# DeltaNet and multiplicative FFN on one Trainium2 core: signs of converted weights taken from VectorE to ScalarE's parametric ReLU, and a new order of the steps

## The chip, the cores and the metric

The kernel runs on one core of a Trainium2 chip. Its time is the device time of one execution in microseconds (us). Five engines matter: TensorE (PE in the profile, its weight loads PEld), VectorE (DVE), ScalarE (ACT), GpSimd (POOL) and SyncE (SP), which issues nearly all DMAs from one queue.

## What is computed

The first half is a delta-rule attention over 768 tokens, for 4 batches and 8 heads of 48 features, with a 48 x 48 state per head. The second half is an FFN without activation functions, over 3072 tokens of 384 features:

```python
k_n = k / (norm(k) + 1e-6)
for t in range(768):
    y[t] = q[t] @ state
    v_old = state^T k_n[t]
    state = state + beta[t] * outer(k_n[t], v[t] - v_old)
x = y as (3072, 384)
out = ((x @ w1) * (x @ w2)) @ w3 @ w_out     # w1, w2: 384 x 1024; w3: 1024 x 1024; w_out: 1024 x 384
```

q, k, v and beta are fp32. The four weight matrices arrive as fp64, eight bytes an element, and the kernel converts them itself.

## The kernel before

**Attention.** The tokens go in 12 chunks of 64. Chunks are taken in pairs j. For each chunk m the program has steps, each a Python generator that issues a few instructions between two `yield`s:

- `k`, `q`, `v` load tiles by tokens, `p` loads permuted tiles of k and q (in eight small DMAs each). `K` and `Q` transpose chunks 0 and 1 on TensorE, `d` transposes the later ones on VectorE.
- `g` sums squares of k for a pair (POOL squares, DVE sums, a small matmul across halves), `N` makes the norms of a pair on DVE (some 14 small instructions) and sends a product across halves, `n` scales v by the norm.
- `s` makes the scores of a chunk (L367, L373) and the matrices U (DVE, L379) and PT. `u` stores U to DRAM in blocks.
- `V` inverts triangular 32 x 32 blocks of a pair: Ub is loaded back (L426), 31 steps of two DVE instructions each (L440, L445), for the first two pairs in PSUM with ScalarE copying in (L434) and out (L449), and Vd is stored. `e` loads the blocks (TT, T22), transposes on DVE (L481), and makes the off-diagonal corner with two sets of matmuls (L498) and ScalarE copies (L514, L525).
- `c` is the serial chain of a chunk: product of the state with k, R = v - that (DVE, L584), product with TT, X (DVE, L594), product with k, new state (DVE, L613 or L615). All these products are L551. `y` makes the outputs (L652) and ScalarE copies them to xT (L673), with a few DMAs.

**Weights.** Each matrix goes in pieces `P`: P0 to P7 are w_out (128 x 384), P8 to P23 w3 (128 x 512), P24 to P29 w1 and P30 to P35 w2. A piece has four steps, one on each of four engines: the load by SyncE into one of five `raw` tiles (a ring), two ScalarE passes (L707 on the high words, L708 on the low words), two VectorE passes (L710 shifts the exponent into place, L711 brings the sign in from the high word), and an integer add on GpSimd (L715). The fifth piece ahead has to be past its add before SyncE can issue the next load.

**FFN.** w3 @ w_out is folded once: `t` transposes a w3 piece on TensorE (L750), ScalarE copies it (L753), `f` multiplies (L759, 128 matmul records), ScalarE copies the result (L766). w_out stands in the tile of w2 (w2s) while it folds. Then, for each pair u of chunks and each of eight column blocks, `a` (and `b` for chunk 0 alone) makes x @ w1, copies it on ScalarE (L791), makes x @ w2 (both L779) and multiplies on VectorE (L795). The product with the folded matrix uses seven block products instead of eight: `T` (weight sums) and `S` (slab sums, L846) run on GpSimd, `o` on TensorE (L874), `x` puts the results together and stores them (L891, L905 to L911).

**Order.** The string `ORDER` lists the steps, one token for each `yield`. The program issues them in this order, and `in_text_order` then ties the instructions of each engine to that order. So ORDER sets the order on each engine, SyncE's queue among them; between the engines only semaphores wait. PSUM has two tiles of two banks (`ps_w`) and four of one bank (`ps_f`), taken in turn; slabs are ten, taken in turn.

Of the kernel before, what the change touches and what calls it, by code (L numbers as in the profile page):

```python
# [8 lines left out]
FP32 = mybir.dt.float32  # L9
# [30 lines left out]
beta k0 P0 g0 P13 P10 P0 k1 P18 beta K0 P0 P0 P12 P13 P13 q0 P10 P18 P10 P10 K0 K0 P13 K0 beta  # L40
K0 g0 g0 q1 P8 P1 P18 g0 P12 P18 P12 K1 g0 k2 K1 K1 K1 g0 g0 P12 Q0 K1 Q0 Q0 g0 Q0 g0 P5 g0 N0
Q0 Q1 P8 P8 s0 t5 Q1 Q1 g1 Q1 Q1 s1 g1 s0 P8 g1 P9 s0 s1 s1 s1 s0 t4 t2 s0 p2 P1 P5 s0 s0 s1 s1
V0 P11 P5 P5 N0 P3 t5 P1 P1 d2 u0 P9 d2 u1 P11 P3 P9 P4 P11 N0 P3 t4 P4 P4 P9 P11 t3 t2 P2 P7
P2 P14 t0 P7 P3 P2 V0 V0 t10 P6 s1 P2 P14 t3 V0 P7 V0 V0 V0 P6 f1 g1 p3 P4 P7 t0 P14 P6 P6 P16
V0 V0 P15 V0 V0 V0 f2 V0 t10 P16 P16 f2 P15 f1 V0 f1 P16 P19 V0 V0 p2 t1 V0 P19 P19 V0 V0 f2 f0
P14 t6 t1 f0 f0 V0 P15 V0 P19 V0 v0 P15 t6 s1 P20 d2 V0 P17 P20 P20 t11 V0 P17 t11 d2 V0 t8 t8
P20 V0 k3 g1 g1 V0 g1 f5 P17 t7 V0 P17 V0 P22 P22 f5 V0 t7 V0 f5 v1 n0 V0 f3 V0 V0 s0 f3 P23
P26 V0 g1 f4 d3 t9 V0 t9 V0 d3 f4 P22 P22 f3 t14 P23 P23 P24 P24 P26 p3 t14 d3 f4 P23 n0 P30
P24 P24 s2 V0 p4 e0 g1 g1 t15 t12 f7 t15 f7 t12 f6 P26 P26 N1 e0 e0 s2 s2 P21 d3 e0 P30 e0 e0
s2 f7 s2 P25 e1 s2 c0 P21 e1 e1 e1 c0 n1 s3 P21 P21 N1 s3 y0 y0 P31 N1 s3 s3 s3 P25 P25 s3 n1  # L50
P31 c0 c0 P25 V1 P30 u2 t13 u3 P32 P30 V1 t13 e1 e1 c1 P31 V1 f6 f6 c1 c1 c1 y1 y0 b1 P32 P32
P32 y1 V1 V1 V1 b0 V1 P31 V1 b0 b2 V1 V1 b1 V1 V1 P27 P27 b1 V1 P27 V1 b1 b2 P29 P29 V1 b3 b3
P29 y1 b3 a03 V1 P28 V1 b3 P27 a01 a02 c1 a03 V1 a00 V1 k4 V1 P29 P28 P28 a01 a00 V1 V1 a00 P28
a02 a05 a00 V1 b5 V1 a05 b6 V1 V1 V1 V1 P35 p4 P35 b6 P33 a07 V1 V1 V1 V1 V1 V1 g2 a07 a04 b5
a04 b7 P33 k5 a06 b4 b7 v2 n2 a01 V1 P35 P33 a06 P34 a03 c1 V1 a03 V1 b2 V1 P35 P33 g2 P34 P34
P34 e2 b2 a01 c2 d4 d4 g2 p5 b4 b0 a04 d4 g2 g2 b0 g2 g2 e2 a07 a06 g2 g2 a04 d4 e2 n2 c2 a07
V2 b4 a06 e2 e2 e2 b5 c2 g2 N2 s4 c2 b4 S0 s4 s4 a02 a02 c2 c2 p5 T b5 T y2 b6 y2 d5 T b7 d5 d5
e3 e3 d5 N2 s4 s4 s4 N2 b7 e3 e3 v3 a05 T u4 a05 s5 b6 S0 s5 s5 S0 s5 s5 n3 o0 x0 e3 e3 s5 c3
n3 c3 S0 u5 S0 S0 S0 S0 o0 S0 S0 S0 S0 c3 c3 o0 V2 y3 x0 o0 V2 S0 V2 S0 V2 V2 V2 o0 V2 y3 V2 k6
x0 S0 g3 c3 g3 g3 S0 g3 V2 v4 x0 o0 V2 V2 V2 y3 V2 a10 a10 x0 x0 k7 x0 o0 V2 x0 x0 a17 V2 V2 V2  # L60
V2 x0 V2 V2 V2 a17 V2 V2 a15 V2 V2 a13 a16 V2 V2 v5 V2 a13 p6 V2 a16 V2 a15 V2 g3 V2 a13 g3 a13
p6 x0 a14 c3 a14 V2 e4 d6 a10 a17 a12 e4 e4 e4 g3 g3 c4 a17 g3 d6 a10 a14 d6 a12 n4 n4 c4 e4 g3
e4 e5 n5 a12 c4 a11 d6 N3 a14 c4 c4 n5 a11 y4 p7 p7 c4 e5 s6 a11 s6 s6 y4 a15 a12 a11 c5 e5 V3
# [26 lines left out]
def kernel(  # L90
# [452 lines left out]
    def chain(c):  # L543
# [30 lines left out]
        R = nv  # L574
# [470 lines left out]
```

## Time and profile before

| what | value |
|---|---|
| median of 3 runs | 609.26 us (609.08 to 610.2) |
| span of the profiled execution, first to last instruction | 607.4 us |
| median of the runs less that span | 1.9 us |
| PE busy | 550.0 us (91%) |
| DVE busy | 364.9 us (60%) |
| ACT busy | 158.9 us (26%) |
| POOL busy | 177.2 us (29%) |
| mean granted TensorE clock | 0.966 |
| DMA | 57.31 MB, 90 GB/s of HBM traffic over the span |

The profiled execution has no time of its own beside its span; the 1.9 us is what lies around the span by the median. "Busy" is time with an instruction in the engine. A group is given as line, engine, operation, output and input tiles with shapes, count, then busy us and mean ns of one, then the idle time of the engine just ahead of them and what ended it. In the chain of waits each row is a start, a length and what was running. In the table by stage each engine's busy us is followed by the number of instructions.

### The profile page before, as it was taken

How to read it: one execution, taken by the hardware profiler on the slowest of the kernel's cores; microseconds unless marked ns; L12 is line 12 of the kernel's file. 1: busy time of each engine (PE TensorE's matmuls, PEld its weight loads, DVE VectorE, ACT ScalarE, POOL GpSimd, SP SyncE). 2: the span in 40 equal slices, each digit the busy share in tenths (PEclk: the TensorE clock that was granted, in tenths of full speed). 3: DMA queues.
4: the chain of work that ended last, by engine and by line, in shares of the span. 5: the costliest groups of instructions: out<-in, count | busy, mean ns of one | idle time of the engine just before them, and what ended most of it. 6: DMA issues, size and time to landing. Idle time of an engine off the chain costs nothing.

```text
span 607.4 us, 19078 instructions
## 1 busy us (share of the span) xinstructions
PE 550.0 (91%) x8188; PEld 383.1 (63%) x8188; DVE 364.9 (60%) x828; ACT 158.9 (26%) x333; POOL 177.2 (29%) x223
## 2 busy tenths in 40 slices
PE   2648789678898999999999989999999999999997
PEld 2545455657777885456964559745588545984477
DVE  3768977466998489765489463894764843311012
ACT  3645534445323111222111221121112012321100
POOL 6554443122255530304420016013053000600041
PEclk9988979669999999999999999999999999999999
DMA  9968998554956347462443534435323040010001
GB/s 192 244 155 226 186 189 173 97 133 94 165 104 88 82 92 120 92 98 39 101 101 73 81 52 87 97 70 103 58 51 84 31 85 5 5 52 13 1 0 52
DMA packets 219507, 57.31 MB, mean 94 GB/s; under 512 B 206656, under 2 KB 212800, under 8 KB 219424
## 3 DMA queue, kind: packets, MB, share of 16 engines
q1 hardware_dynamic: 215232, 55.31, 45.3%
q10 hardware_dynamic: 4192, 0.79, 0.9%
q8 instruction: 64, 1.05, 0.8%
q14 instruction: 19, 0.16, 0.1%
HBM read 43.88 MB, written 11.01 MB: 90 GB/s over the span
## 4 chain that ended last, share of the span: by engine, by line
PE 75%; DVE 8%; DMA 5%; issue 4%; ACT 3%; SPq 3%; ACTq 0%; DVEq 0%
PE ps_f L779 37%; PE ps_f L874 16%; PE ps_w L551 5%; PE ps_f L759 4%; PE ps_w L652 4%; DMA raw<-in_moe_w_dram 3%; PE ps_w L498 3%; PE ps_w L367 2%; DVE tb L440 2%; PE ps_w L373 2%; SPq L230 2%; DVE ps_w L445 2%; DMA ktok<-in_k_dram 1%; ACT xT L673 1%; PE ps_f L750 1%
## 5 line engine op out<-in xcount | busy, mean ns | idle before, releaser
L779 PE MATMUL ps_f<-xT,w2s 128*128 128x512 f32 (+1 forms) x336 | 133.7, 544 | 1.6 <-issue 1.5
L779 PE MATMUL ps_f<-xT,w1s 128*128 128x512 f32 (+1 forms) x336 | 128.7, 533 | 4.5 <-DVE ab L795 2.0
L846 POOL TENSOR_TENSOR ab<-ab 128x256 f32<-128x256 f32 x96 | 67.2, 729 | 195.0 <-DVE ab L795 171.0
L779 PEld LDWEIGHTS ps_f<-xT,w1s 128*128 128x128 f32 x336 | 63.0, 190 | 60.3 <-issue 52.0
L779 PEld LDWEIGHTS ps_f<-xT,w2s 128*128 128x128 f32 x336 | 63.2, 193 | 56.2 <-issue 52.3
L791 ACT COPY ab<-ps_f 128x512 f32<-128x512 f32 (+1 forms) x56 | 28.4, 525 | 172.7 <-PE ps_f L779 161.4
L874 PE MATMUL ps_f<-w,ab 128*128 128x192 f32 x376 | 66.5, 330 | 0.0
L874 PEld LDWEIGHTS ps_f<-w,ab 128*128 128x128 f32 x376 | 61.1, 190 | 4.4 <-issue 3.5
L795 DVE TENSOR_TENSOR ab<-ab,ps_f 128x512 f32<-128x512 f32 (+1 forms) x56 | 33.2, 605 | 49.1 <-PE ps_f L779 49.0
L440 DVE TENSOR_TENSOR tb<-Vb,Ub 128x31 f32<-128x31 f32 (+15 forms) x124 | 46.0, 371 | 15.5 <-DMA Ub<-Ud 12.1
L759 PE MATMUL ps_f<-w2s,w3T 128*128 128x384 f32 x128 | 48.4, 535 | 5.7 <-ACT w3T L753 5.0
L445 DVE TENSOR_TENSOR Vb<-Vb,tb 128x31 f32<-128x31 f32 (+15 forms) x124 | 47.2, 381 | 4.3
L874 PE MATMUL ps_f<-room,ab 128*128 128x192 f32 x272 | 47.9, 330 | 1.1 <-DVE room L905 1.1
L874 PEld LDWEIGHTS ps_f<-room,ab 128*128 128x128 f32 x272 | 44.1, 190 | 1.9 <-issue 1.5
L673 ACT COPY xT<-ps_w 48x256 f32<-48x256 f32 x96 | 30.4, 365 | 48.1 <-PE ps_w L652 47.5
L759 PEld LDWEIGHTS ps_f<-w2s,w3T 128*128 128x128 f32 x128 | 26.2, 211 | 24.2 <-ACT w3T L753 5.5
L270 POOL TENSOR_TENSOR sq<-ktok 128x384 f32<-128x384 f32 x24 | 20.9, 875 | 61.4 <-DMA ktok<-in_k_dram 30.1
L367 PE MATMUL ps_w<-KQ 48*64 48x128 f32 x384 | 31.3, 308 | 3.9 <-issue 2.0
L379 DVE TENSOR_TENSOR U<-ps_w,wt 128x512 f32<-128x512 f32 x24 | 16.6, 690 | 29.9 <-PE ps_w L373 28.6
L715 POOL TENSOR_TENSOR w<-w,raw 128x512 uint32<-128x512 uint32 x16 | 20.7, 1299 | 43.6 <-DVE w L711 18.6
L373 PE MATMUL ps_w<-KQ 48*64 48x64 f32 x768 | 32.1, 242 | 0.3 <-issue 0.3
L537 POOL TENSOR_TENSOR vtok<-vtok,n 128x384 f32<-128x384 f32 x24 | 20.1, 851 | 41.0 <-DMA vtok<-in_v_dram 26.8
(109 smaller groups left out, 676.4 us busy)
## 6 DMA issues: line engine op xcount, KB each, us to landing
raw<-in_moe_w_dram SPq DMA_DIRECT2D x16, 512.0 KB, 6.2
vtok<-in_v_dram SPq DMA_DIRECT2D x24, 192.0 KB, 4.3
raw<-in_moe_w_dram SPq DMA_DIRECT2D x24, 192.0 KB, 4.0
out_dram<-osb SPq DMA_DIRECT2D x46, 96.0 KB, 2.2
ktok<-in_k_dram SPq DMA_DIRECT2D x44, 96.0 KB, 3.9
raw<-in_moe_w_out_dram SPq DMA_DIRECT2D x8, 384.0 KB, 4.8
Ud<-U SPq DMA_DIRECT2D x48, 64.0 KB, 2.1
Ub<-Ud SPq DMA_DIRECT2D x6, 512.0 KB, 3.4
```

The source lines that it names most:

```text
L367: pe.matmul(ps[half(z), 0, n : n + 128], lhsT=x[:, 0, :], rhs=x.rearrange("p j t -> p (j t)"), start=True, stop=True,)
L373: pe.matmul(ps[half(z ^ j), 1, n + C * j : n + C * j + C], lhsT=x[:, 0, :], rhs=x[:, j, :], start=True, stop=True,)
L440: dve.tensor_tensor(out=tv, in0=V[:, 0 : s + 1, s : s + 1].to_broadcast([P, s + 1, n]), in1=U[:, s, s + 1 : BS].unsqueeze(1).to_broadcast( ...
L445: dve.tensor_tensor(out=o, in0=o, in1=tv, op=ALU.subtract)
L551: pe.matmul(out(ps, r, h, z), lhsT=lhs(r, h, z), rhs=rhs(r, h, z), start=True, stop=True,)
L673: act.copy(out=xT[f, p:NP:2, b : b + NR, cc, :].rearrange("p a r t -> p r a t"), in_=pyv[f, z, b : b + NR],)
L759: pe.matmul(ps[:, 0:DM], lhsT=w3Ts[jc, kc // 4][:, kc % 4 * P : kc % 4 * P + P], rhs=wo[:, kc], start=(kc == 0), stop=(kc == KF - 1),)
L779: pe.matmul(ps[:].rearrange("p b c t -> p b (c t)"), lhsT=w[:, m, js], rhs=x[:, m, :, c0:c1].rearrange("p b c t -> p b (c t)"), start=(m = ...
L791: act.copy(out=t, in_=ps)
L795: dve.tensor_tensor(out=t, in0=t, in1=ps, op=ALU.mult)
L846: pool.tensor_tensor(out=o_, in0=x_, in1=y_, op=op)
L874: pe.matmul(ps[b][:, b, :], lhsT=abs_[u, HF * f + i][:, t0 : t0 + P], rhs=ws_[w][:, i], start=first and i == 0 and (b == 0 or n == "F"), s ...
```

## The change

The ScalarE pass over the high words used the absolute value, scaled by 2^-112; a VectorE pass then put the sign bit in. Now the pass is a parametric ReLU with slope -2^32 for negative inputs: a negative number becomes a positive one whose exponent has one more bit set, and the shift by three places that follows moves that bit into the sign's place. The sign pass is dropped. In `chain` the lookups of KQ and v are made where they are first used, so that the first product of a chunk may be issued ahead of the load of its v. ORDER is new throughout; the steps in it are the same.

```diff
 ORDER = """
-beta k0 P0 g0 P13 P10 P0 k1 P18 beta K0 P0 P0 P12 P13 P13 q0 P10 P18 P10 P10 K0 K0 P13 K0 beta
-K0 g0 g0 q1 P8 P1 P18 g0 P12 P18 P12 K1 g0 k2 K1 K1 K1 g0 g0 P12 Q0 K1 Q0 Q0 g0 Q0 g0 P5 g0 N0
...
+V0 beta q1 beta beta k0 K0 K0 K0 K0 K0 Q1 g0 g0 q0 Q1 Q1 k1 g0 g0 K1 K1 Q1 K1 Q1 g0 g0 g0 g0 g0
+g0 N0 K1 P10 P10 K1 s1 N0 P10 P13 Q0 P13 P9 P10 t2 P13 P13 P0 P9 P0 N0 P9 P12 P12 P12 P12 P0 P0
...
 def chain(c):
-        TT, nv, KQ = TTs[c % 2], vtoks[c], KQs[c]
+        TT = TTs[c % 2]
...
-        R = nv
         if c > 0:
+            KQ = KQs[c]
...
+            nv = vtoks[c]
...
+        else:
+            R = vtoks[c]
...
-        act.activation(out=dst, in_=hi.bitcast(FP32), func=ACTF.Abs, scale=2.0**-112)
+        act.activation(
+            out=dst, in_=hi.bitcast(FP32), func=ACTF.Prelu, scale=2.0**-112, alpha=-(2.0**32)
+        )
         act.activation(out=lo, in_=lo, func=ACTF.Copy, scale=2.0**-29)
         yield
         dve.tensor_scalar(out=du, in0=du, scalar1=3, scalar2=None, op0=ALU.logical_shift_left)
-        dve.scalar_tensor_tensor(
-            out=du, in0=hi, scalar=0x80000000, in1=du, op0=ALU.bitwise_and, op1=ALU.bitwise_or
-        )
         yield
         pool.tensor_tensor(out=du, in0=du, in1=lo, op=ALU.add)
```

What the new order does on each engine up to the corner of chunk 2, as the lists of instructions show it:

- SyncE: q1 and k1 go first, ahead of all weights; then P10, P13, P9, P0, P12, one permuted set, P15, k2, P11, P8, P14, P18, P4, P3, P1, P2, U of chunk 0, P5, P6, U of chunk 1, P7, P19, and then the reload Ub. Before, w_out and w3 pieces stood ahead of k1, q0 and q1, and Ub came ahead of the last w_out piece (P6).
- TensorE: nine transposes of w3 pieces come ahead of the first fold (six before); six more and seven and a half folds (f6's second half is left) come ahead of e0's first product in both. After it the order is e0, c0, y0, f6's second half, e1, scores of chunk 3, c1, y1, and then b. Before, f6's second half stood inside c1.
- VectorE: the norms of pair 0 stand ahead of the first conversion, and the four score products of chunks 0 and 1 ahead of P11's. V0 follows P19's shift.
- ScalarE: V0's two copies out stand next to each other. Before, a copy of a transposed w3 piece (t7) stood between them.

More of the change, by code (lines that the diff above doesn't have):

```diff
@@ L39 @@
 ORDER = """
-beta k0 P0 g0 P13 P10 P0 k1 P18 beta K0 P0 P0 P12 P13 P13 q0 P10 P18 P10 P10 K0 K0 P13 K0 beta
-K0 g0 g0 q1 P8 P1 P18 g0 P12 P18 P12 K1 g0 k2 K1 K1 K1 g0 g0 P12 Q0 K1 Q0 Q0 g0 Q0 g0 P5 g0 N0
[L42 to L63, printed above, removed]
@@ new lines @@
+p2 P9 t1 Q0 Q0 d2 P15 d2 k2 P11 t5 Q0 Q0 P15 s0 P15 P15 s0 s0 s1 s1 s0 s0 s0 s1 s1 s1 g1 t7 g1
+g1 g1 P11 P11 P11 P8 P8 P8 P8 P14 P14 P14 P18 P18 P18 t1 t2 t4 P14 t6 P18 t5 P4 P4 P3 P3 P3 t10
+P1 P3 s0 P4 P4 P1 P1 P1 t6 t7 t3 t4 P2 P2 u0 P2 P2 t0 t0 f2 P5 P5 P5 P6 P6 P6 P6 t10 f0 u1 P5 P7
+P7 P7 P7 f2 f2 P19 t3 f1 f1 V0 P19 P19 P19 V0 V0 V0 V0 V0 V0 V0 V0 V0 V0 V0 s1 s1 f0 P17 t11 f3
+t11 f3 v0 V0 P17 P17 P17 P20 P20 f0 V0 V0 t9 P20 P20 f1 t12 t12 V0 V0 V0 V0 P16 P16 V0 V0 P16
+P22 P22 P22 f3 P22 t9 f5 f5 t14 P16 t8 t8 f4 f4 V0 V0 p2 d2 f5 t14 f7 V0 d2 P23 P23 V0 V0 V0 V0
@@ new lines @@
+V5 V5 V5 V5 x3 a40 a40 x3 a43 a46 a43 a46 a42 a42 a42 V5 V5 V5 V5 n11 n11 V5 V5 V5 V5 V5 V5 V5
+V5 V5 V5 V5 V5 V5 V5 V5 a42 a40 a45 V5 V5 V5 a40 a45 a41 a41 a44 a44 a43 a43 v10 a46 n10 a47 V5
+e10 c9 e10 e10 e10 a41 a41 N5 a46 c10 N5 e10 o4 a47 n10 c10 e10 c10 a45 c10 y10 y10 a47 c10 e11
+e11 e11 a45 a47 e11 o4 c10 c11 c11 e11 x4 o4 e11 c11 x4 x4 S4 S4 S4 S4 o4 S4 S4 S4 S4 S4 S4 S4
+c11 y11 o4 x4 S4 o4 x4 y11 S4 S4 S4 S4 x4 y11 a52 a52 x4 x4 x4 o4 x4 a56 a56 a55 a57 a55 a57 a55
+a55 a54 a54 a52 a52 x4 a54 a50 a50 a50 a54 a50 S5 a51 a56 a56 a51 a51 a51 S5 S5 a57 a53 a57 a53
@@ L86 @@
+a53 a53 S5 o5 S5 S5 S5 S5 x5 o5 S5 S5 S5 S5 o5 S5 S5 S5 S5 x5 o5 x5 o5 x5 o5 x5 x5 x5 o5 x5 x5
+x5 x5 x5 x5 x5
 """
```

52 lines of the change are left out of this document (30 added, 22 removed).

## The prediction

> **What bounds the kernel now.** I read the 40 slices of the page first, then the busy time by stage, then the chain that ended last in order of time, and last the groups of instructions and the timelines of VectorE, GpSimd and SyncE up to 200 us.
>
> The slices (15.2 us each), busy tenths; PEclk is the granted TensorE clock:
>
> ```profile
> PE   2648789678898999999999989999999999999997
> DVE  3768977466998489765489463894764843311012
> PEclk9988979669999999999999999999999999999999
> DMA  9968998554956347462443534435323040010001
> ```
>
> From slice 12 on TensorE is full at full clock. Before that it has gaps, and VectorE and the DMA engines are the busy ones. I cut the span at four events: the first corner product of chunk 0 (step e0, L498, at 105.28), the first matmul of a·b (step b1, L779, at 139.22), the corner of chunk 2 (181.50) and the start of the last output products (585.16):
>
> ```profile
> core 0: us, PE busy (x) PEld busy (x) DVE busy (x) ACT busy (x) POOL busy (x), PEclk, DMA share, GB/s
> 0.00:105.28 105.28, 73.60 (x700) 50.67 (x700) 75.46 (x173) 50.30 (x92) 52.73 (x61) 0.92 0.89 193
> 105.28:139.22 33.94, 24.73 (x865) 20.40 (x864) 17.63 (x29) 15.21 (x30) 6.88 (x7) 0.70 0.58 127
> 139.22:181.50 42.28, 37.75 (x301) 31.22 (x296) 36.88 (x93) 16.33 (x39) 14.52 (x15) 1.00 0.61 117
> 181.50:585.16 403.66, 395.74 (x6229) 262.95 (x6230) 231.16 (x526) 76.15 (x170) 94.08 (x129) 1.00 0.36 67
> 585.16:607.40 22.24, 18.20 (x113) 17.91 (x111) 3.81 (x8) 0.96 (x2) 8.97 (x13) 1.00 0.11 35
> ```
>
> TensorE idles 31.7 + 9.2 + 4.5 us in the first three stages and 7.9 us in the 404 us after. So the change can win only before 181.5, where all weights are converted, and what it wins there shifts the rest to the left.
>
> The removed pass is L711; L707 is the ScalarE pass whose function changes:
>
> ```profile
> L711 DVE SCALAR_TENSOR_TENSOR w<-raw,w 128x512 uint32<-128x512 uint32 x16 | 13.2, 827 | 0.5
> L711 DVE SCALAR_TENSOR_TENSOR w2s<-raw,w2s 128x384 uint32<-128x384 uint32 x8 | 7.5, 942 | 0.3
> L711 DVE SCALAR_TENSOR_TENSOR w2s<-raw,w2s 128x512 uint32<-128x512 uint32 x6 | 6.1, 1020 | 0.2
> L711 DVE SCALAR_TENSOR_TENSOR w1s<-raw,w1s 128x512 uint32<-128x512 uint32 x6 | 5.6, 938 | 0.2
> L707 ACT ACTIVATE w<-raw 128x512 f32<-128x512 f32 x16 | 10.8, 673 | 17.5 <-DMA raw<-in_moe_w_dram 17.3
> ```
>
> In the chain, at the places that the new order rearranges, and on GpSimd, where the last piece of w_out becomes ready:
>
> ```profile
> 91.17 0.59 ACT Vb L449
> 105.35 0.73 PE ps_w L498 x50
> 130.28 4.36 PE ps_f L759 x8
> 134.64 1.12 PE ps_w L551 x64
> ```
>
> ```profile
> 56.72 1.01 POOL L715 TENSOR_TENSOR w2s<-w2s,raw 128x384 uint32<-128x384 uint32 x1 [3.55 <-DVE w2s L711]
> ```
>
> **The removed pass by itself.** 36 instructions, 32.4 us of VectorE, 32.5 in the stage table of that line alone: 22.9 up to 105.28, 4.4 from there to 139.22, 5.2 after. Only part of it lies on the path: VectorE idles 29.8 us in the first stage and 16.3 in the second. In each piece it also lies between load and use, so a piece of 512 columns is ready 0.69 us sooner (1.65 where the pass was stretched).
>
> **The new function on ScalarE.** No pass is added; 36 instructions run another function. The trace has no such function. Nearest rows: absolute value 673 ns and copy with a scale 667 ns for 128x512, so I take 0; bounded by 0.09 us less (the plain copy from PSUM, 587 ns) and by twice the price, 36 x 0.66 = 24 us on an engine idle for 55 of the first 105 us, where a piece comes 0.66 us later: at most 1 us at the end. The program has one table load in both orders (1.28 us); a second one is excluded by that. [...]
>
> **The new order, stage 1 (to e0).** Two paths meet at 105.28.
>
> TensorE path: folding w3·w_out is 128 matmuls. Both orders do the first 16 to 20 of them and then need the eighth piece of w_out. By the issue sizes, SyncE loads ahead of it 8 pieces of 384 KB, eight of 512 KB, five k/q tiles, one permuted set, and U stored and reloaded; after, nine of 512 KB and no reload of U (it comes later): equal in KB. So w_out is complete at about 57.7 in both. From there before has 100 matmuls and nine transposes to e0 and takes 47.5 us, of which 4.3 wait for a piece transposed late (until 76.99), some 2 for others, and 2.5 go to slow matmuls (32 in 13.17 us, 0.41 each, against 8 in 2.75, 0.34). After it has 100 matmuls and six transposes, as three pieces more are transposed earlier: 100 x 0.335 + 6 x 0.53 = 36.7, so 94.4. The last piece that it waits for (P23) comes 4.4 MB after w_out's, at 195 GB/s 23 us, ready by 81; it is used at about 89.
>
> VectorE path: inverse V0 starts later, because SyncE loads P7 and P19 ahead of U: w_out's last piece lands at 53.5, 1 MB more is 5.1 us, so 59 (52.7 before). Its 62 instructions take 21.3 us and 2 of gaps; four shifts (0.45) and two transposes (0.65) stand among them: ends at 85.4 (84.7 before, with the sign passes among them). Then the two copies back: before, the second stood on ScalarE behind a copy that waited for TensorE and ended at 91.76; now they are adjacent: 86.6. Store 2.9, reload 4.4 (before, eight permuted loads, 5.5 us of SyncE, stood between): 94. The norms of pair 1 end about there too (they wait for a matmul that now stands at 89, then 4.4 us), then one transpose and one shift, 1.1, and e0's own 0.7: 95.7. The sum gives 96; I put 2 us on it for hand-offs that I cannot place: 98, a gain of 7.3.
>
> **Stage 2 (e0 to b1), 33.9 us.** A serial chain: corner products and copies 4.0; c0's first product 1.9, X 1.0, y0 2.2, state product 1.1; then the second half of fold 6, 2.7 to 4.4, beside the state's copies (1.9); e1 0.8, scores of chunk 3 3.4, c1 1.95, R 0.95, e1's second half and copy 2.0, product 1.1, X 1.0, y1 2.3, state 1.1. With 3.5 for the fold this is 28.3, and 29 with hand-offs. Before, the fold stood between c1's first two products (4.36 us in the chain above, R being ready 3.3 earlier), and five sign passes, 4.4 us, stood on VectorE among X, S and R. Gain 4.9. The last shift and add of w1's third piece (0.4 + 1.3) lie beside y1 and the state product (3.4); if that cover goes, they cost 1.7. The second pair's conversions queue on ScalarE behind corner copies; nobody waits for those until 10 us later.
>
> **Stage 3 (to 181.5).** TensorE-bound: 1.49 us for each half of a·b, 26 of them before, 29 after ahead of e2. Work 40.9 and 44.3; before took 42.3. Best 2 us gained; a loss of 2 if VectorE, which now drains more halves behind V1, holds a bank; I take 1. V1 itself starts 14 us sooner and is as long (six shifts and four products among its 23.3 us, 26.6 against 26.9).
>
> **Stages 4 and 5.** The same work on a full engine; every chain product still has an output product (2.6 us) or another beside it. 0, with 3 either way. The order of SyncE's other loads (k, v, permuted) changes, at a DMA share of 0.36; 0. The last products start behind a53 instead of a57: 0 to 1.
>
> Sum: 7.3 + 4.9 + 1 = 13.2. The profiled span is 607.4 and the median of the runs 609.26; the 1.9 us around the span stay. 609.3 - 13.2 = 596.1.
>
> **The rivals.**
>
> *Slower: the weight ring runs dry.* The first conversion's shift now stands on VectorE behind the norms of pair 0, and P11's behind the four score products of chunks 0 and 1. SyncE can run only five pieces ahead and stands still at the sixth, with all loads behind it. In before the first shift runs at 8.1 and those scores end at 38.6, with 1 to 3 us of waits between. For it: k0 landed at 10.9 and k1 at 16.3, behind weights. Against: k1 and q1 are now issued first, five pieces and 2 MB of k and q are in flight meanwhile, 22 us of transfer. I get the first shift at 20 and P11's at 38, where the DMA engines are about to go idle. Each idle microsecond goes to everything behind it; past 13 us (scores ending at 51) the gain is gone. With 20 us: 616. Chance 0.14.
>
> *Less: TensorE runs cold.* In stage 2 the granted clock was 0.70, and the 8 fold matmuls there took 0.545 us each. If the folds run at 0.41 as in 77 to 90, stage 1 takes 100 x 0.075 = 7.5 more: 603.6. For it: gaps remain while pieces arrive. Against: with nine pieces transposed ahead (six before), the folds run with few gaps. [...] Chance 0.22, for all gains of 2 to 8 us.
>
> *More: nothing waits.* Stage 1 ends at 94.4, stage 2 takes 27.5, stage 3 and 4 give 2 and 3: 21.4, 588. Chance 0.11.
>
> *It is hidden anyway*, a change within 0.2% (1.2 us, about what a measurement of this kernel tells apart): 0.03. That the pass is not gone is excluded by the program's list of instructions.
>
> **How the numbers follow.** Forecast 0.50 (588 to 601), cold 0.22, more 0.11, same 0.03, slower 0.14. Faster: 0.83. The range reaches from 587 to 609, which leaves out most of the slower case and a little below. The likeliest case's own range is 589 to 601.
>
> **What would show it.** Right: e0's first product at 94 to 100, b1 29 us later, V0 ending no later than 87, and stage 4 as long as before. Wrong: DMA idle in 23 to 45 us, shifts waiting on VectorE behind scores until 50, folds at over 0.4 us each, or a 36-fold ScalarE group above 0.7 us.

## The result, and the profile after

The changed kernel takes 607.19 us (median of 17 runs, 603.7 to 613.24). The kernel before, on the same chips, took 609.26 (607.36 to 612.13, 17 runs). The ratio is 0.9954, 95% interval 0.9937 to 0.9971: 2.8 us faster by the ratio, 2.1 by the medians. The forecast was a gain of 13.2. The sign was right, the size was not, and experiments found where the rest went: to the order, not to the parametric ReLU.

The slices of the page, for TensorE, VectorE and the granted clock (compare those of before):

```profile
PE   4558997869998999999899998999899999999997
DVE  2551886538975369665597555793464863310112
PEclk9657999759999999999899999999899999999999
```

VectorE's busy time fell from 364.9 to 334.0 us. But the granted clock is lower early on (slices 2 to 4 read 6, 5, 7 where before had 9, 8, 8), and in the rear slices 20 and 29 lost a tenth. The same cut into stages, by the same five events:

```profile
core 0: us, PE busy (x) PEld busy (x) DVE busy (x) ACT busy (x) POOL busy (x), PEclk, DMA share, GB/s
0.00:98.88 98.88, 71.15 (x652) 48.12 (x653) 53.98 (x146) 49.51 (x92) 46.45 (x57) 0.83 0.83 189
98.88:135.74 36.86, 28.45 (x977) 23.49 (x977) 15.88 (x27) 17.23 (x37) 12.86 (x13) 0.67 0.69 142
135.74:176.25 40.51, 40.51 (x243) 34.91 (x241) 34.74 (x92) 15.05 (x34) 18.39 (x18) 0.96 0.76 136
176.25:585.00 408.75, 396.51 (x6214) 263.13 (x6214) 225.64 (x521) 76.44 (x170) 88.54 (x123) 0.99 0.36 66
585.00:607.20 22.20, 18.15 (x111) 17.68 (x109) 3.72 (x8) 0.96 (x2) 8.96 (x13) 0.98 0.11 35
```

Stage 1 gained 6.4 us (105.28 to 98.88). Stage 2 lost 2.9 (33.94 to 36.86), although VectorE has less to do in it. Stage 3 gained 1.8. Stage 4 lost 5.1 (403.66 to 408.75), and it had three halves of a·b fewer to do (three were left at its start, six before; 1.49 us each), so at equal work it lost 9 to 10. The profiled spans differ by 0.2 us only: 607.4 and 607.2.

The ScalarE pass and the shift behind it cost what was expected (line numbers are three to five higher than before):

```profile
L710 ACT ACTIVATE w<-raw 128x512 f32<-128x512 f32 x16 | 10.7, 669 | 4.1 <-DMA raw<-in_moe_w_dram 3.9
L715 DVE TENSOR_SCALAR w<-w 128x512 uint32<-128x512 uint32 x16 | 9.4, 606 | 9.7 <-ACT w L710 9.7
```

The absolute value took 673 ns for this shape, the parametric ReLU takes 669: term zero.

Stage 2 has holes in its chain of waits, in order of time (start, length, what):

```profile
106.78 0.85 PE ps_w L655 x25
107.63 0.73 issue
108.36 1.32 PE ps_w L655 x36
...
118.83 0.80 issue
119.63 0.27 PE ps_w L373
...
121.61 0.90 PE ps_w L498 x36
122.52 2.43 issue
124.95 0.48 PE ps_w L498 x15
...
134.48 0.70 issue
135.18 0.63 PE ps_w L551 x17
```

"issue" means that TensorE waited for nothing that the profile shows. The holes fall in the middle of a set of products (36 of e1's second set, then 2.43 us of nothing, then more of the same set), so no data and no other engine is in sight as what was missing. Before has such holes too: in TensorE's list of waits "issue" adds up to 3.4 us in its stage 2, and to 4.8 us in that of after. The third part of the page names something that can be missing, the queue that brings instructions:

```profile
q8 instruction: 64, 1.05, 0.8%
```

64 packets of 1.05 MB together are 16.4 KB each (16,384 bytes for every one of them in the trace). The page counts 8188 matmuls and 8188 weight loads, 16,376, and 64 x 256 is 16,384: by these counts one packet is a block of 256 TensorE instructions, 64 bytes each. By the packet times in the trace each of these four holes ends 1.40 to 1.50 us after such a packet has landed. And counted over all of TensorE's records (matmuls, loads, and the 165 waits and drains in its queue), each stands ahead of record number 256 k + 193, with k a whole number: at the same place in a block each time. Where the packets come most densely they start some 4.1 us apart (3.43 at the least). A product of the chain (64 matmuls, 64 loads) takes 1.06 us of engine time (286.82 to 287.88 in after) but half a block of code, so a run of such products uses a block in about 2.1 us, twice as fast as blocks come at 4.1 us (an estimate from these numbers). That is the theory the experiments test: **theory A, code supply**. The rival, **theory B**, is the prediction's own picture: engine times, data and semaphores, with TensorE's code always there.

### The profile page after: what moved, and what is told of

It reads as the page before. It is cut to its first block, busy times and chain, and to the rows that moved or that the text cites. A ratio compares the mean times of both kernels' runs of the same rounds, so it can differ in the third digit from the quotient of the medians.

```text
span 607.2 us, 18976 instructions
## 1 busy us (share of the span) xinstructions
PE 554.8 (91%) x8188; PEld 387.3 (64%) x8188; DVE 334.0 (55%) x792; ACT 159.2 (26%) x333; POOL 175.2 (29%) x223
## 3 DMA queue, kind: packets, MB, share of 16 engines
q8 instruction: 64, 1.05, 0.8%
## 4 chain that ended last, share of the span: by engine, by line
PE 83%; issue 6%; DVE 4%; ACT 3%; DMA 2%; POOL 1%; ACTq 0%; SPq 0%; DVEq 0%; POOLq 0%
PE ps_f L781 41%; PE ps_f L876 19%; PE ps_w L551 5%; PE ps_f L761 5%; PE ps_w L655 4%; PE ps_w L498 2%; PE ps_w L367 2%; PE ps_w L373 2%; PE ps_f L752 1%; DMA ktok<-in_k_dram 1%; PE ps_w L876 1%; POOL w L717 1%; DMA raw<-in_moe_w_out_dram 1%; ACT raw L713 1%; DMA TT<-Vd 1%
## 5 line engine op out<-in xcount | busy, mean ns | idle before, releaser
L781 PE MATMUL ps_f<-xT,w2s 128*128 128x512 f32 (+1 forms) x336 | 131.5, 536 | 0.3 <-issue 0.3
L781 PE MATMUL ps_f<-xT,w1s 128*128 128x512 f32 (+1 forms) x336 | 130.1, 537 | 0.0
L781 PEld LDWEIGHTS ps_f<-xT,w1s 128*128 128x128 f32 x336 | 64.4, 193 | 55.7 <-issue 51.2
L781 PEld LDWEIGHTS ps_f<-xT,w2s 128*128 128x128 f32 x336 | 62.6, 190 | 55.7 <-issue 52.2
L876 PE MATMUL ps_f<-w,ab 128*128 128x192 f32 x376 | 68.6, 336 | 1.2 <-issue 0.7
L876 PEld LDWEIGHTS ps_f<-w,ab 128*128 128x128 f32 x376 | 62.5, 194 | 4.5 <-issue 3.4
L876 PE MATMUL ps_f<-room,ab 128*128 128x192 f32 x272 | 50.4, 339 | 1.1 <-DVE room L907 0.8
L761 PE MATMUL ps_f<-w2s,w3T 128*128 128x384 f32 x128 | 46.7, 523 | 1.7 <-ACT w3T L755 1.7
L445 DVE TENSOR_TENSOR Vb<-Vb,tb 128x31 f32<-128x31 f32 (+15 forms) x124 | 45.0, 363 | 4.3
L440 DVE TENSOR_TENSOR tb<-Vb,Ub 128x31 f32<-128x31 f32 (+15 forms) x124 | 44.4, 358 | 5.2 <-DMA Ub<-Ud 1.6
L876 PEld LDWEIGHTS ps_f<-room,ab 128*128 128x128 f32 x272 | 45.6, 196 | 2.4 <-issue 1.6
L379 DVE TENSOR_TENSOR U<-ps_w,wt 128x512 f32<-128x512 f32 x24 | 16.5, 689 | 36.2 <-PE ps_w L373 36.1
```

The lines of the kernel that those rows point to most:

```text
L440: dve.tensor_tensor(out=tv, in0=V[:, 0 : s + 1, s : s + 1].to_broadcast([P, s + 1, n]), in1=U[:, s, s + 1 : BS].unsqueeze(1).to_broadcast( ...
L445: dve.tensor_tensor(out=o, in0=o, in1=tv, op=ALU.subtract)
L761: pe.matmul(ps[:, 0:DM], lhsT=w3Ts[jc, kc // 4][:, kc % 4 * P : kc % 4 * P + P], rhs=wo[:, kc], start=(kc == 0), stop=(kc == KF - 1),)
L781: pe.matmul(ps[:].rearrange("p b c t -> p b (c t)"), lhsT=w[:, m, js], rhs=x[:, m, :, c0:c1].rearrange("p b c t -> p b (c t)"), start=(m = ...
L876: pe.matmul(ps[b][:, b, :], lhsT=abs_[u, HF * f + i][:, t0 : t0 + P], rhs=ws_[w][:, i], start=first and i == 0 and (b == 0 or n == "F"), s ...
```

## The experiments

Stage times are from one profiled execution each (e0 is the first corner product, b1 the first matmul of a·b, "corner 2" the corner of chunk 2). The ratio is to before in the same session, where its median was 608.2 to 609.9 us, so differences by the ratios and by the medians are not quite the same:

| kernel | e0 | b1 | corner 2 | end | runs | median us | ratio to before (95%) |
|---|---|---|---|---|---|---|---|
| before | 105.3 | 139.2 | 181.5 | 607.4 | 17 | 609.26 | |
| after | 98.9 | 135.7 | 176.3 | 607.2 | 17 | 607.19 | 0.9954 (0.9937 to 0.9971) |
| e1 old order, ReLU | 102.1 | 135.0 | 173.5 | 600.3 | 6 | 602.23 | 0.9910 (0.9884 to 0.9937) |
| e2 new order, sign pass | 109.6 | 144.4 | 189.8 | 617.3 | 6 | 619.63 | 1.0207 (1.0174 to 1.0240) |
| e3 new front, old rear | 102.1 | 134.7 | 178.4 | 613.8 | 6 | 616.86 | 1.0150 (1.0115 to 1.0186) |
| e4 old front, new rear | 102.5 | 138.2 | 177.4 | 606.5 | 12 | 608.09 | 0.9992 (0.9961 to 1.0023) |
| e5 five steps exchanged | 99.8 | 133.0 | 174.9 | 608.0 | 12 | 609.99 | 1.0014 (0.9990 to 1.0039) |
| e6 old order, three exchanged | 103.2 | 133.2 | 172.8 | 602.1 | 12 | 603.64 | 0.9899 (0.9866 to 0.9933) |
| e7 small products thrice | 100.7 | 152.8 | 192.5 | 624.5 | 2 | 625.19 | 1.0248 (1.0197 to 1.0299) |
| e8 more large matmuls | 102.6 | 143.3 | 186.2 | 621.9 | 2 | 622.44 | 1.0203 (1.0151 to 1.0255) |
| e9 folds as cover | 100.3 | 136.4 | 181.0 | 603.7 | 10 | 605.50 | 0.9931 (0.9907 to 0.9955) |
| e10 b1 ahead of y1 | 101.8 | 130.9 | 173.2 | 597.1 | 10 | 603.38 | 0.9902 (0.9866 to 0.9938) |
| e11 y first | 100.6 | 135.0 | 177.0 | 608.6 | 12 | 611.99 | 1.0035 (1.0005 to 1.0065) |
| e12 new front, old rear, mended | 99.6 | 134.2 | 175.2 | 598.9 | 6 | 602.36 | 0.9886 (0.9844 to 0.9929) |
| e13 new rear, less y | 98.0 | 129.7 | 174.6 | 588.5 | 6 | 590.72 | 0.9693 (0.9653 to 0.9734) |
| e14 old rear, less y | 100.0 | 135.0 | 176.2 | 590.0 | 5 | 590.94 | 0.9692 (0.9651 to 0.9733) |

One profile of stage 2 is not sharp: the eight kernels with the new order in it and its work unchanged (after, e2, e3, e5, e11 to e14) took 36.9, 34.8, 32.6, 33.2, 34.4, 34.6, 31.7 and 35.0 us, a mean of 34.1. The four with the old order (before, e1, e4, e6) took 33.9, 32.9, 35.7 and 30.1, a mean of 33.2.

**The two halves of the change apart (e1, e2).** e1 is the changed kernel with the ORDER of before:

```diff
-ORDER = """ V0 beta q1 beta beta k0 K0 ...        (the new order)
+ORDER = """ beta k0 P0 g0 P13 P10 P0 k1 ...       (the order of before)
```

> The new pass (parametric ReLU, no sign pass) under the order of before. Theory A (code supply: TensorE's instructions arrive in blocks of 256, one per 4 to 5 us when it is starved, so the stretches dense in small products keep their length whatever VectorE does): the stage from the first corner product to the first a*b product stays at 33 to 35 us, only the stage before it shortens, by 2 to 4 us; the time is 605 to 608. Theory B (the sign passes lay on the path, and the new order spoils what their removal gives): the passes of the chain go from the time, 597 to 602.

e2 keeps the new order and puts the old pass back:

```diff
-        act.activation(
-            out=dst, in_=hi.bitcast(FP32), func=ACTF.Prelu, scale=2.0**-112, alpha=-(2.0**32)
-        )
+        act.activation(out=dst, in_=hi.bitcast(FP32), func=ACTF.Abs, scale=2.0**-112)
...
+        dve.scalar_tensor_tensor(
+            out=du, in0=hi, scalar=0x80000000, in1=du, op0=ALU.bitwise_and, op1=ALU.bitwise_or
+        )
```

> The new order with absolute value and the sign pass kept. Theory A: V0 ends some 4 us later (six sign passes of 0.69 us among or ahead of its steps), the corner of chunk 0 comes at 102 to 104 instead of 98.9, the next stage is as long as in the changed kernel (36 to 38 us), and the time is 609 to 613. Theory B: what is lost is lost by the order alone, and the pass is worth its 10 us or more on top: 615 or more. If the pass is hidden in this order: 607.

Without the pass the old order takes 602.23 us, 0.9 per cent less than before (5.5 us by the ratio) and 5 us less than the changed kernel (2.7 by the ratios, whose intervals just touch). The new order with the sign pass takes 619.63. So the pass is worth 5 to 7 us in the old order and 12 to 15 in the new one (619.63 - 607.19 by the medians, 0.0253 of before by the ratios), and the new order costs 3 to 5 us without the pass and 10 to 13 with it. The gain that was measured is the ReLU's, less what the new order takes back. These two runs tell the ReLU from the order, and nothing yet for theory A: e2 came out as B had it, and e1 with a stage 2 of 32.9 us and 602.2 us in all just outside what either said.

**Which part of the order (e3, e4, e12).** Each takes the first tokens of one order and the rest in the other's, cut behind the first matmuls of the third pair's a·b:

```diff
-ORDER = new order
+ORDER = first 776 tokens of the new order, the remaining ones in the order of before     (e3)
+ORDER = first 785 tokens of the order of before, the remaining ones in the new order     (e4)
```

> The new pass; new order up to the end of the second group of output products (o1), then what is left in the order of before. Theory A: the changed kernel led by 6.3 us there and lost 5.9 of it later, to waits for code and to half clock after them in the new rear; with the old rear the lead is kept: 602 to 605. Rival C (the rear loses to something that the front leaves behind, transfers or buffers that run ahead): still 606 to 608.

> The new pass; order of before up to the same point (end of o1), then the rest in the new order. Theory A: the front is that of the first run of this set, the rear loses 3 to 6 us against it: 609 to 614. Rival C: the rear is no slower by itself, and the time is that of the first run of this set within 1 us.

e3 missed, through its own joint. The list of TensorE's waits behind the corner of chunk 2 starts with it:

```profile
PE ps_f L781 <- DVE osb L907: 11.4, 1, 11.4
```

The joint put VectorE's next sums behind a load of k that had just been issued; TensorE waited 11.4 us for VectorE once. e3 says nothing on the orders. e4 has no such wait, and its 608.09 against e1's 602.23 puts a loss of 5.9 us (5.0 by the ratios, whose intervals do not touch) on the rear. e12 is e3 with the joint mended:

```diff
-... V3 V3 k8 g4 g4 g4 g4 k9 d8 v7 a20 a20 a23 V3 x1 V3 x1 n7 a27 a24 d8 a26 V3 ...
+... V3 V3 k8 k9 v7 a20 a20 a23 V3 x1 V3 x1 n7 a27 a24 a26 V3 ... V3 g4 g4 g4 g4 g4 d8 d8 g4 a26 ...
```

> Again the new order up to a20 and the order of before behind it, but at the joint the squares of k and two transposes of VectorE go behind 25 steps of V3, so that VectorE does not wait for a load of k just issued. With parametric ReLU. If the new order's loss lies in its rear (old front with new rear 608.1, old with old 602.2, new with new 607.2), new front with old rear gives 602.2 + 607.2 - 608.1 = 601.3; I expect 600 to 604, and no wait of over 3 us at the joint. If the loss lies in the new front or at its end, 605 to 609.

602.36, as worked out (601.3). The four combinations are then 602.2 (old, old), 608.1 (old, new), 607.2 (new, new) and 602.4 (new, old): the front makes no difference to the total that these runs can tell, the new rear costs 5 to 6 us with either (4 to 5 by the ratios). So of the prediction's gains the front as a whole brings nothing over the old one once the pass is gone, and the rear, put at 0, takes back nearly all of the ReLU's gain.

**Is it the code? Stage 2 (e7, e8).** Two additions of the same engine time, one with much code and one with little:

```diff
-            for r in range(NR):
+            for _ in range(3 if c < 2 else 1):          # e7, products of the chain
+              for r in range(NR):
...
-        for kc in range(KF):
+        for n in range(KF * (3 if jc == 6 else 1)):     # e8, the fold
+            kc = n % KF
```

> The changed kernel with the five products of chunks 0 and 1 (L551) issued three times each into the same place, all of them between e0 and b1: 640 more matmul records and as many weight loads, 5 blocks of 256 instructions. By engine time each product is 1.06 us, so ten more are 10.6 us. Theory A (code supply): e0 to b1 takes 5 blocks x 4.1 to 5.0 = 20 to 25 us longer than 36.9, so 57 to 62. Theory B (a serial chain of engine times, as in the prediction): 10.6 longer, 47.5; if all of it runs at half clock, up to 52.

> The changed kernel with 16 more fold matmuls (32 records of 128x384) in the second half of fold 6, between e0 and b1; they write what was there. The same 10.7 us of engine time as the ten extra products of the run before, at 0.335 us a record, but in 64 instructions, a quarter of a block. Theory A (code supply): while they run, the next blocks of code land, and holes and slow clock behind them shrink: e0 to b1 grows by 3 to 9 us from 36.9, to 40 to 46. Theory B (serial engine times): 10.7 longer or more, 47.6 to 54 (at the 0.57 that fold 6 showed, 18 us).

The tables of stage 2, e7 first, and the instruction queue's row in that stage of e7:

```profile
100.66:152.83 52.17, 36.15 (x1616) 31.32 (x1616) 15.19 (x26) 18.84 (x40) 12.30 (x12) 0.80 0.48 103
```

```profile
102.58:143.31 40.73, 34.45 (x1008) 25.91 (x1009) 15.47 (x26) 16.26 (x34) 12.27 (x12) 0.87 0.56 115
```

```profile
q8 instruction: 12, 0.20, 1.7%
```

e7's stage 2 takes 52.2 us: 15.3 more than the profile of after, 18.1 more than the mean of 34.1, where engine time is 10.6 and A asked for 20 to 25. It runs 3232 instructions, 12.6 blocks, in 52.2 us, 4.13 us a block, with 16 us of TensorE idle, 13.1 of them put down to "issue": about the rate at which blocks come. A's figure took 4.1 to 5.0 us for each added block; as the whole stage ends at 4.13 a block, some of its time before had not been code's. e8's takes 40.7: 3.9 more than the profile of after, 6.6 more than the mean, for 10.7 us of work; the granted clock rose from 0.67 to 0.87. In this stage equal engine time cost 18 us as small products and 7 as large ones. Theory B, which asked for 10.6 and at least 10.7, falls: e8 is well below it, and the 52 us that it allowed e7 were for half clock throughout, where 0.80 was granted. (e8's added matmuls do not write what was there: by then piece P31 has taken the place of parts of w_out's pieces P2 and P3 in w2s, which they read again. In number and shape they are as described, and TensorE ran all 40 records of that half without a wait, in 13.89 us.)

**Is it the code? The rear.** The same two runs show what its holes are, without having been made for it. TensorE's rear in after, y5, y7 and y8 (start, length, form, and in brackets the idle time ahead):

```profile
293.10 0.42 PE L655 MATMUL ps_w<-KQ,S 48*48 48x64 f32 x10
295.25 0.55 PE L655 MATMUL ps_w<-KQ,S 48*48 48x64 f32 x22 [1.74 <-issue]
295.73 4.53 PE L876 MATMUL ps_f<-room,ab 128*128 128x192 f32 x16
...
375.42 0.33 PE L655 MATMUL ps_w<-PT,X 64*48 64x64 f32 x9 [2.05 <-issue]
...
434.54 0.33 PE L655 MATMUL ps_w<-KQ,S 48*48 48x64 f32 x7 [1.49 <-issue]
434.80 4.55 PE L876 MATMUL ps_f<-w,ab 128*128 128x192 f32 x16
```

In e7, which has 1280 instructions more ahead of this, exactly five blocks:

```profile
314.44 0.55 PE L656 MATMUL ps_w<-KQ,S 48*48 48x64 f32 x22 [1.75 <-issue]
...
393.82 0.33 PE L656 MATMUL ps_w<-PT,X 64*48 64x64 f32 x9 [1.52 <-issue]
...
452.64 0.33 PE L656 MATMUL ps_w<-KQ,S 48*48 48x64 f32 x7 [1.20 <-issue]
```

In e8, which has 64 more, a quarter of a block:

```profile
286.46 0.27 PE L373 MATMUL ps_w<-KQ 48*64 48x64 f32 x2 [1.17 <-issue]
293.06 0.47 PE L551 MATMUL ps_w<-X,ktok 64*48 64x48 f32 x18 [2.29 <-issue]
```

With five whole blocks added, the holes stand ahead of the same records (22, 9 and 7 before the end of a set); with a quarter of a block they stand elsewhere. All of them are again ahead of records 256 k + 193. In these three runs a hole belongs to a place in the code, not to the data. Which places they are has its price too: behind the corner of chunk 2 TensorE's waits for "issue" add up to 12.0 us in e8, where after has 8.3, so that over the whole run the two additions cost nearly the same, 18.0 us (e7) and 15.3 (e8). After a hole the next 16 output products can take 4.5 us for 2.87: behind y5's hole in after they took 4.53, and the granted clock in the trace is 0.50 from 295.73 to 299.14 and 1.00 on both sides. The spells at 0.50 in the traces of before and after are 3.41 us long or multiples of that, up to 10.24 us in before and 23.89 in after, but for one that the end of the trace cuts short in each. In after y8's hole of 1.49 us was followed by such a spell (435.67 to 439.08), y7's of 2.05 was not (1.00 from 374 to 380), and neither was one of 1.82 at the first place, in e12 (16 output products in 2.87 us behind it, clock 1.00 from 175.24 to the end). So in this kernel a hole of 1.5 to 2.1 us was followed by half clock at times and at times not; what decides it no run shows.

**Can another order cure the rear (e5, e6, e11)?** All three exchange neighbouring TensorE steps, so that a large step stands between small ones:

```diff
 e5 (new order), TensorE
-... o0.4 o0.5 c3.5 y3 ...   c5.5 y5 o1.6 ...   c7.5 y7 o2.5 ...   a37.3 e9.3 y8 ...   y9 o3.5 ...
+... o0.4 c3.5 o0.5 y3 ...   c5.5 o1.6 y5 ...   c7.5 o2.5 y7 ...   e9.3 a37.3 y8 ...   o3.5 y9 ...
 e6 (order of before, with ReLU), TensorE
-... y2 b6.3 ...   o1.3 y5 ...   c6.5 a23.3 ...
+... b6.3 y2 ...   y5 o1.3 ...   a23.3 c6.5 ...
 e11 (new order), TensorE; on VectorE c5.6 goes ahead of three steps of V3
-... o0.5 c3.5 y3 o0.6 ...   c5.5 y5 o1.6 c6.1 o1.7 ...   c7.5 y7 o2.5 c8.1 o2.6 ...   a37.3 e9.3 y8 ...
+... y3 o0.5 c3.5 o0.6 ...   y5 o1.6 c5.5 o1.7 c6.1 ...   y7 o2.5 c7.5 o2.6 c8.1 ...   e9.3 a37.3 y8 ...
```

> The changed kernel with five TensorE steps of the rear exchanged with their neighbour, so that a step of few large matmuls (an output product, a half of a*b) stands between two steps of many small ones: o1.6 ahead of y5, o2.5 ahead of y7, o3.5 ahead of y9, c3's last product ahead of o0.5, e9's first set ahead of a37's second half. Nothing else moves and no instruction is added or removed. Theory A (code supply: TensorE's code comes in blocks of 256 instructions, at best one per 3.6 to 4.2 us, so dense stretches of small products run dry, and half a clock follows each hole): the holes ahead of or in y5 (1.74), y7 (2.05) and y8 (1.49) shrink to under 0.7, the output products behind them run at 2.8 us for 16 and not 4.5, and the stretch from the corner of chunk 2 to the end falls from 431.0 to 421 to 427 us; time 598 to 603. Theory B (the rear loses for another reason, such as banks held by VectorE): the stretch stays at 429 to 433, time 605 to 609.

> The parametric ReLU in the order of before (602.2 us), with three TensorE steps exchanged with their neighbour: b6's second half ahead of y2, y5 ahead of o1.3, a23's second half ahead of c6's last product. Theory A (code supply): the holes that stood there in that run (2.01 in y2, 2.07 behind c6's product) go, with up to 1.7 us of slow matmuls behind each: 596 to 600 us. Theory B: 601 to 604.

> The changed kernel with the rear's TensorE order changed at four places, so that y comes earlier and not later: y3, y5 and y7 each go ahead of the chain's last product of the same chunk, with an output product between the two (o0.5, o1.6, o2.5) and another behind (o1.7, o2.6); e9's first set goes ahead of a37's second half; the new state of chunk 6 goes ahead of three steps of V3 on VectorE. Theory A (code supply makes the rear's holes, and what took their place in the run with five exchanged steps were y's and the state's lateness, which this order avoids): the holes in y5 and y7 (1.7 and 2.1) shrink below 0.7 with no wait for S or xT of over 1 us in their place; from the corner of chunk 2 to the end 424 to 428 us against 431.0; time 600 to 604. Theory B (VectorE's order sets the pace there, and a hole only fills time that TensorE would wait anyway): 429 to 433, time 605 to 609.

The holes in y5, y7 and y8 went, in e5 and in e11, and nothing was gained: 609.99 and 611.99 us. Other waits stand in their place. In e5:

```profile
297.29 1.50 PE L551 MATMUL ps_w<-S,KQ 48*64 48x48 f32 x57 [2.80 <-DVE S L618]
```

```profile
381.98 4.47 PE L781 MATMUL ps_f<-xT,w1s 128*128 128x512 f32 x6 [2.19 <-DMA xT<-xT]
```

and in e11:

```profile
302.63 4.54 PE L876 MATMUL ps_f<-w,ab 128*128 128x192 f32 x16 [5.36 <-DVE osb L907]
```

y moved back made its copies and DMAs late for the next pair's a·b; y moved forward met VectorE's sums of the results, queued among V3's steps. Old holes were traded for new waits, most of them with slow matmuls behind (six of 512 columns in 4.47 us, 16 output products in 4.54).

The first of these waits is not the price of a filled hole. The output product o1.6 adds into a bank that VectorE has to read between o1.5 and o1.6. Moved ahead of y5, o1.6 also came ahead of that reading sum, which now waits for it:

```profile
292.33 0.56 DVE L907 TENSOR_TENSOR room<-room,ps_f 128x384 f32<-128x384 f32 x1 [3.40 <-PE ps_f L876]
```

In after the same sum, at 291.54, waits for nothing. The new state stands behind it in VectorE's order; 3.40 us sooner it would have been there before c6 asked for it (an estimate from these rows). So e5 sums one term too many and does not compute the kernel's result. Neither does e11: o1.6 and o2.6 stand ahead of their sums, and c8's first product takes y7's tile ahead of y7's copies. Both show that a hole can be moved; the price of filling it they do not show cleanly.

e6 does, and its result is the kernel's. Its 603.64 us are not told apart from e1: the two holes that it aimed at went, "issue" behind the corner of chunk 2 fell from 5.0 to 1.4 us, and a wait of 2.3 us for VectorE's sums and one of 1.5 us for the state came. These runs told against the simple form of theory A, that filling the holes returns their time.

**The rear with less code (e13, e14).** So the code was taken away and the order left alone. Both leave out the products of PT with X in y for chunks 4 to 11, 1024 instructions:

```diff
-            for r in range(NR if mode == 0 else 0):
+            for r in range(NR if mode == 0 and c < 4 else 0):
```

> The changed kernel, which leaves out the products of PT with X in y for chunks 4 to 11 (8 times 64 matmul records and as many weight loads, 4 blocks of code; by engine time 8 x 1.1 = 8.8 us); order and all else are those of the changed kernel. To be compared with the next run, which leaves out the same in the order of before from a20 on. Theory A (the new rear loses 4.8 us, 607.2 against 602.4, because its code comes too late where small products are dense): with half of y's code gone, the two differ by less than 2 us; this run at 592 to 596. Theory B (VectorE's order or another wait in the new rear): they differ by 4 to 6 us still; this run at 597 to 600.

> The kernel with the new order up to a20, the order of before behind it and the joint mended (602.4 us), which leaves out the products of PT with X in y for chunks 4 to 11, as the run before. By engine time 8.8 us less: 593 to 595; both theories expect this, and differ in how far it lies from the run before (A less than 2 us, B 4 to 6).

590.72 and 590.94 us: the 4.8 us between the two rears are gone. The old rear gained 11.4 us and the new one 16.5, for 8.8 us of engine time in both. VectorE's order and work were untouched, and a TensorE that is faster by 8.8 us would sooner wait for VectorE than before, so VectorE's order is not a likely reason for the slower rear. Code is what A said: 60 blocks where there were 64.

TensorE's lists of waits bear it out in part. Behind the corner of chunk 2 the waits put down to "issue" add up to 8.3 us in after, 8.2 in e2 and 7.2 in e4, which have the new rear; to 3.8 in before, 5.0 in e1 and 6.5 in e12, which have the old one; and to 3.0 in e13 and 3.1 in e14. So some 3 of the 5 us stand in the holes. Of the rest, after has two spells of half clock in its rear (3.41 us each) and e12 none, but e4, with the new rear, has none either. And no run took the same engine time out of large matmuls. That code is the whole of the rear's loss is argued, not shown.

**Stage 2 rewritten (e9), and one filler (e10).** With theory A in hand, large steps were put among the small ones of stage 2:

```diff
 e9 (order of before, with ReLU), TensorE
-... t14 s2.1 g1 t15 t12 f7.1 f7.2 f6.1 e0.3 e0.5 s2.4 c0.1 e1.3 s3.1 N1 y0 s3.4 c0.3 t13 e1.5 c1.1 f6.2 c1.3 y1 b1.1 ...
+... t14 g1 t15 t12 e0.3 f7.1 e0.5 f7.2 c0.1 f6.1 e1.3 c0.3 y0 s2.1 s2.4 e1.5 c1.1 s3.1 t13 N1 s3.4 f6.2 c1.3 b1.1 y1 ...
 e10 (order of before, with ReLU)
-... c1.3 y1 b1.1 ...      SyncE: u2 u3 P32 V1 y0
+... c1.3 b1.1 y1 ...      SyncE: u2 y0 u3 P32 V1
```

> The parametric ReLU in the order of before (602.2 us; e0 at 102.1, b1 at 135.0, corner of chunk 2 at 173.5), with the steps around stage 2 rewritten by hand: V0's two copies adjacent on ScalarE, its store and the reload of the blocks ahead of other DMAs on SyncE, e0 ahead of the last three fold halves, which stand between e0's, e1's and c0's products, and the scores of chunk 2 behind y0; b1's first matmuls ahead of y1. Nothing is added or removed. Theory A (code supply: 256 instructions per 4.1 us at best, 27.7 us for the 6.75 blocks of stage 2, so large matmuls put among the small ones cost next to nothing): e0 at 92 to 96, b1 at 126 to 131, and the time 594 to 599. Theory B (stage 2 is a serial chain of engine times): the three fold halves, 7.9 us, lengthen stage 2 by as much as e0 came earlier; b1 at 133 to 137, 600 to 604 us.

> The parametric ReLU in the order of before, with two moves alone: b1's first matmuls ahead of y1 on TensorE (where it waited 1.24 us for X), and for that y0's DMAs ahead of the store of chunk 3's U on SyncE. Both theories: the wait for X is covered, b1's second half starts 1.0 to 1.3 us sooner, 600.5 to 602 us against 602.2.

e9 missed. e0 came at 100.3 and not at 92 to 96, because the blocks that VectorE transposes for it landed late (VectorE waited 6.44 us for them, TensorE then 5.39 us at that place), and from e0 to the end of y1 it took 39.9 us against e1's 32.9: of 9.4 us of work moved in (three fold halves and b1's first matmuls) only 2.4 were hidden. 605.5 us is above e1. But e9 is no clean test of the idea. In its order c1 forms R ahead of n1, which scales the v that R takes, so the result is not the kernel's. And on GpSimd n1 now waits for R, and the add of the last w3 piece, P21, stands behind n1:

```profile
125.14 0.95 POOL L537 TENSOR_TENSOR vtok<-vtok,n 128x384 f32<-128x384 f32 x1 [21.74 <-DVE R L585]
```

That add started at 126.05 (at 111.89 in e1), and TensorE waited 1.58 us for it. What e9 takes without this no run shows. e10's b1 starts at 130.9 in what was the wait for X, as expected, but its 603.38 us (598.89 to 608.16) can't be told apart from e1's 602.23.

e1 and e12, both at 602.3 us, are the fastest versions that compute the whole result; e6 and e10 can't be told from them.

## Why the prediction was right or wrong, by its steps

- *The removed pass and the new function.* Right: 36 passes gone, VectorE busy 30.9 us less (not 32.4, as the shift that stays takes longer: 606 ns for 128x512 in w where it took 422), ScalarE's term 0.
- *Stage 1.* Right within its error, in part by luck: e0 at 98.88 (predicted 98), the shifts at 19.4 and 38.3 (20 and 38), the folds at 0.333 us where 0.335 was used. But V0 ended at 88.6 and not at 85.4 (nor by 87), and the folds ended at 98.3 and not at 94.4, with 4.5 us of waits among them that the sum of 36.7 did not have; the 2 us for hand-offs took most of this in. Over the other eight profiles of this front without the sign pass e0 lies between 98.0 and 102.6, 100.4 on average; with the old order and no pass (e1, e4, e6, e10) it is 102.4. So of some 5 us gained the pass alone brings 3. The slower rival, the ring running dry, did not come.
- *Stage 2.* This step failed. The sum of 28.3 was a chain of engine times, taken from the chain of waits, and it left out two things. First, TensorE's code: the new stage has 977 matmuls and as many loads, 7.6 blocks. At the 4.13 us of e7's stage 2 that is 31.5 us, more than the 29 of the forecast (an estimate that leaves out what has landed ahead). The 6.75 blocks of the old stage would take 27.9, so not all of its 33.9 us was code's. Second, the new order puts half of the scores of chunk 2, 48 matmuls, behind e0, inside the stage, and the sum has no term for them. (The other 64 of the 112 matmuls more are c1's last product, which the sum has as its last 1.1.) Forecast 29, measured 36.9, mean of eight profiles 34.1. The granted clock fell from 0.70 to 0.67; the rival "TensorE runs cold" had that, but looked for it in the folds of stage 1, which ran at 0.333 us each. The measured gain lies in the 2 to 8 us that this rival was given, but not through slow folds.
- *Stage 3.* Right in size: 1.8 us gained, predicted 1, on TensorE's 100% busy. The work was put too high: 44.3 us with 29 halves of a·b, where the stage with all 29 in it took 40.5, as a half took some 1.36 us there and not 1.49.
- *Stages 4 and 5, put at 0.* This step failed too, and it was the dearer one. "every chain product still has an output product (2.6 us) or another beside it" counts engine time; the new order leaves less large work between small products (y5 and c6's first product have one output product between them, two before; y8 stands directly behind e9's first set, before it was a37's second half), and holes stand there that fall at places of the code. That the loss lies in the rear's order is shown twice: e4 against e1 and after against e12 give 5 to 6 us by the medians, 4 to 5 by the ratios. That it is code is supported by e13 against e14, which differ by nothing once half of y's code is gone, and by the sums of "issue", which hold some 3 us of it. What the time of one hole is worth is not shown: e6, and less cleanly e5 and e11, lost holes and got waits for VectorE and xT in their place, and no order was found that keeps the new front's lead in the new rear.
- *The sum.* 7.3 + 4.9 + 1 + 0 = 13.2 against 6.4 - 2.9 + 1.8 - 5.1 = 0.2 in the profiled pair. The sign was carried by the pass alone: 5 to 7 us in the old order.

Signs of both failures stood in the profile of before. The third part of its page has 64 packets on the instruction queue, and TensorE's list of waits has 2.3 us of "issue" inside y in the rear and 3.4 us of it in stage 2. The prediction has no term for either.

## What to carry to other kernels

Where TensorE runs many small matmuls, count its instructions in each stage (a matmul and its weight load are two) and divide by the stage's time: here some 256 per 4.1 us came in the densest stage (e7's). That a stage near that rate has little to gain from a faster VectorE is the author's estimate: stage 2 in the old order took 33.9 us in before and 32.9, 35.7 and 30.1 without the sign passes (e1, e4, e6), which is no sharp test of it. A reorder that moves small products together can cost more than the waits that it removes (the new rear cost 5 to 6 us here), so judge an order and a cheaper instruction apart before putting both into one change. An "issue" hole in the middle of a set of equal matmuls is worth a look at the instruction queue's packets: here four in stage 2 of after ended 1.40 to 1.50 us after one had landed.

## What the runs showed of the hardware that was not expected

- TensorE's code arrived in blocks of 16,384 bytes, 256 instructions each by these counts: 64 packets for 16,376 instructions in before and after, 69 in e7 (1280 more), 65 in e8 (64 more), 60 in e13 and e14 (1024 fewer). By the packet times two blocks start at least 3.57 us apart in before and 3.43 in after, and some 4.1 in dense stretches (4.13 a block over e7's stage 2).
- Counted with all of TensorE's records, its queue's waits and drains among them, packet number i (the first is 0) starts no sooner than after 256 i + 148 of them in after (149 in before), and as long as it has not landed TensorE gets no further than 256 i + 449 in both. So the lead was 1.2 blocks, some 300 instructions: by an estimate from after's rows 2.5 us of small products at 1.06 us for 128 (286.82 to 287.88), but 26 us of output products at 2.80 us for 32 (287.90 to 290.70), so that large ones between would give the lead back.
- The holes reach 2.43 us in after (ahead of 124.95) and stood at fixed places in the code, each ahead of one of the records 256 k + 193 (ten of over 0.4 us in after, six in before); the 64 instructions that e8 adds far ahead moved them to others.
- A parametric ReLU with a slope of -2^32 cost ScalarE 669 ns for 128 x 512 in after, as the absolute value did in before (673).
